# Weight places of 4128 instead of 4096 bytes in an attention and two-MLP kernel

## The chip, the cores and the metric

The kernel runs on one NeuronCore of a Trainium2 chip. The metric is the device time of one execution in microseconds. Three runs of the kernel before took 950.89, 951.58 and 952.81 us; the median is 951.58 us.

## What is computed

Linear attention with exponential features, and two MLPs behind it, all float32. The matmuls of the MLPs split each operand in two parts (high and low) that TensorE takes as `float32r`, and add three products.

```python
def phi(x):                                   # d_feat = 128
    proj = x @ w_phi
    proj = proj - max(abs(proj), axis=-1)
    return concat([exp(proj), exp(-proj)])
q_p, k_p = phi(q), phi(k)                     # q, k, v: 4 x 8 x 576 x 64
kv = einsum('bhsf,bhsd->bhfd', k_p, v); z = sum(k_p, axis=2)
x = einsum('bhsf,bhfd->bhsd', q_p, kv) / (einsum('bhsf,bhf->bhs', q_p, z) + 1e-6)
x = x.transpose(0, 2, 1, 3).reshape(2304, 512)
x = ((x @ w1) * (x @ w2)) @ w3 @ w_out        # d_ff = 1024
x = square(maximum(x @ w_in, 0)) @ w_out2     # d_ff = 2048
```

## The kernel before

Three stages follow each other on TensorE: attention (about the first 190 us), the first MLP (to about 550 us) and the second MLP (to the end). The 2304 rows are worked in four blocks of 512 columns (one for each batch) and one block of 256 columns, the tail rows of all batches (`mains`, `tail`, lines 787 to 789). Attention writes its rows to HBM, and the MLP blocks are loaded from there.

**The matmuls of the MLPs.** `passes` (line 155) gives the three pairs: high with high, low with high, high with low. `wide` (line 175) makes 12 matmuls: for each of four 128-row slices of the input three passes, with a slice of a weight tile as the stationary operand and a tile `c` of the input (512 columns) as the moving one. The first MLP runs `wide` for `pa` and `pb`, and `fold_in` (line 877) makes 12 matmuls `yp` with the folded weight `w3o` stationary and the gated product `g` moving. `w3o` is the product of w3 and w_out, 24 matmuls `pf` for each of eight slices (line 840, class `Fold`). One loop of the first MLP is `pa`, `pb` and the `yp` of the step before; there are two groups of four steps on each block. The second MLP runs `wide` for `ph` (a column tile of w_in stationary) and `last_product` (line 895) for `op`: there the squared activation `r` is stationary and the tile of w_out moves. One loop is `ph` of step j and `op` of step j - 1, 16 loops on each block.

**Behind a `ph`** ScalarE takes the relu (`t`, line 1035), VectorE the square (line 1037), ScalarE the high part of `r` (line 1043), VectorE the low part (line 1045); `op` needs `r` one loop later. The input tiles `c` and `y` are split the same way (`split`, lines 144 and 145).

**Where tiles lie.** All tiles lie in SBUF, with 128 partitions each, and sizes here are bytes of one partition. A tile of a weight is `[2, 512]` in 4 bytes, so 4096: the high part, then the low part. There are 20 places on the left side (`LEFT`, pool `units`, tag "u") and 12 on the right (`RIGHT`, pool `late`, tag "w"). `unit` (line 64) and `lunit` (line 708) hand them out; `take` (line 718) picks a side and falls to the other where the first has no free place, and `give`, `tick` and `home` keep the count. The same places also hold x and y tiles on their way from and to HBM. The `c` tiles have places of their own (`place`, line 67, pool `mid`, behind the left places); the `g` and `r` tiles share a tag of `late`, behind the right places. In the program as it is built, left place k begins at byte 43648 + 4096k, the `c` places at 125568 + 4096k, right place k at 159712 + 4096k, and the three places of `g` and `r` at 217056, 221152 and 225248. Counted modulo 64 that is 0, 0, 32 and 32. Between the left and the right pools 1376 bytes are free. In attention the matmuls `pk` (line 246) have a `c` place (offset 0) stationary and `wbd`, on the right at 189472 (offset 32), moving.

In the second MLP the w_in tiles (even numbers of `w_w2`) lie left, and the w_out tiles (odd numbers) lie right, but for the numbers 11, 13, 15 and 31, which lie left. At 668.88 us `op` takes number 11, at 674.42 number 13.

The order of the instructions on each engine is written out by hand (`START`, `SLOT`, the loops under `manual_schedule`).

Of the kernel before, what the change touches and what calls it, by code (L numbers as in the profile page):

```python
# [17 lines left out]
P = 128  # L18
C = 4
TAIL = 64  # L20
LEFT = 20
RIGHT = 12

# [18 lines left out]
def attention_then_mlps(ctx: ExitStack, tc: tile.TileContext, q, k, v, w_phi, w1, w2, w3, wo, wi2, wo2, out):  # L44
# [15 lines left out]
    units = ctx.enter_context(tc.tile_pool(name="units", bufs=1))  # L60
    mid = ctx.enter_context(tc.tile_pool(name="mid", bufs=1))
    dram = ctx.enter_context(tc.tile_pool(name="dram", bufs=1, space=bass.MemoryType.DRAM))

    def unit(dtype, shape, name):
        return units.tile([P] + shape, dtype, tag="u", bufs=LEFT, name=name)

    def place(i, name):

# [59 lines left out]
    def decode_splitting(src, name, got, tile_of=unit):  # L128
        w = []
        yield from decoding(src, name, w)  # L130
        dst = tile_of(F32R, [2, 512], f"w_{name}")
        yield
        nc.scalar.activation(dst[:, 0], w[0], AF.Copy)  # L133
        yield
        nc.gpsimd.tensor_tensor(out=dst[:, 1], in0=w[0], in1=dst[:, 0].bitcast(F32), op=ALU.subtract)  # L135
        got.append(dst)
# [38 lines left out]
    def wide(ps, n, w, cs, kks=range(KD)):  # L175
# [8 lines left out]
        (b, i): dram.tile([P, 2, C * P], F32, name=f"x_hbm_{b}_{i}") for b in range(B) for i in range(KD // 2)  # L184
    }
    xt = unit(F32, [KD, B * TAIL], "xt")
    y_hbm, x_in, y_in = {}, {}, {}

    def load_x(b):
        if b == B:  # L190
            x_in[b] = [xt[:, kk, :] for kk in range(KD)]
            return
        x_in[b] = []
        for i in range(KD // 2):
            xu = unit(F32, [2, C * P], f"x_{b}_{i}")
            nc.sync.dma_start(xu, x_hbm[b, i])
            x_in[b] += [xu[:, 0, :], xu[:, 1, :]]


    with ExitStack() as actx:  # L200
# [346 lines left out]
        def plan(kind, i):  # L547
            got = []
            if kind == "w3":
                return got, decoding(*w3_of(i), w3s), 0  # L550
            if kind == "w12":
                src, name = w12_of(i)
                return got, decode_splitting(src, name, w12, lambda *a: take(*a, side="u")), 1
            side = "w" if i % 2 else "u"
            return got, decode_splitting(w2_of(i), f"w2_{i}", got, lambda *a: take(*a, side=side)), 1
# [133 lines left out]
        with tc.manual_schedule(engines=mine):  # L689
            for entry in START:  # L690
                name, t = entry.split("/")
# [11 lines left out]
    late = ctx.enter_context(tc.tile_pool(name="late", bufs=2, side="right", reuse_waits="tile"))  # L703
# [2 lines left out]
    pre = ctx.enter_context(tc.tile_pool(name="pre", bufs=4, space=PSUM, reuse_waits="tile"))  # L706

    def lunit(dtype, shape, name, tag="w", bufs=RIGHT):
        return late.tile([P] + shape, dtype, tag=tag, bufs=bufs, name=name)

    def bank_of(pool, tag, name):
# [1 line left out]


    free = {"u": LEFT - 18, "w": RIGHT}
    home, given = {}, []

    def take(dtype, shape, name, side="w"):

        tag = side if free[side] else "uw".replace(side, "")  # L720
        assert free[tag] > 0, name
        free[tag] -= 1
        t = (lunit if tag == "w" else unit)(dtype, shape, name)
        home[t.name] = tag
        return t

    def give(*ts):
        given.extend(home.get(t.name, "u") for t in ts)

    def tick():  # L730
        while given:
# [60 lines left out]
    def load_x_at(b):  # L792
        if b == B:
            x_in[b] = [xt[:, kk, :] for kk in range(KD)]
            return []
        us = [take(F32, [2, C * P], f"x_{b}_{i}_{len(blocks)}") for i in range(KD // 2)]
        for i, xu in enumerate(us):
            nc.sync.dma_start(xu, x_hbm[b, i])
        x_in[b] = [xu[:, s, :] for xu in us for s in range(2)]
        return us  # L800
# [9 lines left out]
    class Fold:  # L810
# [22 lines left out]
        def product(self):  # L833
            self.pf = pf = bank_of(pre, "pre", f"pf_{self.kc}")
            for g in range(2):
                t = self.t[g]
                for j in range(4):
                    sl, wj = slice(j * P, (j + 1) * P), wos[4 * g + j]
                    for n, (a, c) in enumerate(passes((t[:, 0, sl], t[:, 1, sl]), (wj[:, 0], wj[:, 1]))):
                        nc.tensor.matmul(pf, a, c, start=g + j + n == 0, stop=g == 1 and j == 3 and n == 2)  # L840
            give(*self.t)
            if self.kc == NG - 1:
                give(*wos)
# [13 lines left out]
    def evict_first(b, n, yp):  # L857
        us = [take(F32, [2, n], f"y_{b}_{i}") for i in range(KD // 2)]
        for i, y in enumerate(us):
            nc.scalar.copy(y[:, 0, :], yp[2 * i][:, 0:n])  # L860
            nc.vector.tensor_copy(y[:, 1, :], yp[2 * i + 1][:, 0:n])
            y_part[b, i] = dram.tile([P, 2, n], F32, name=f"y_part_{b}_{i}")
            nc.sync.dma_start(y_part[b, i], y)
        give(*us)
# [52 lines left out]
    with tc.manual_schedule(engines=mine):  # L917
# [5 lines left out]
        for s, (grp, at, k) in enumerate(steps):  # L923
# [7 lines left out]
            b, n = blk.b, blk.n  # L931
# [16 lines left out]
            if s == 0:  # L948
                g = first["g"]
            else:  # L950
                pa = bank_of(pre, "pre", f"pa_{b}_{c}")
                wide(pa, n, w12[2 * c], blk.cs)
                a_sb = lunit(F32, [512], f"a_{b}_{c}", "t", 2)
                nc.scalar.copy(a_sb[:, 0:n], pa[:, 0:n])  # L954
                pb = bank_of(pre, "pre", f"pb_{b}_{c}")
                wide(pb, n, w12[2 * c + 1], blk.cs)
                if at == B:
                    give(w12[2 * c], w12[2 * c + 1])
                if k == HG - 1:
                    col_split(x_in[nb_], nn, f"c{s}_{nb_}", [1, 2])  # L960
                g32 = lunit(F32, [512], f"g32_{b}_{c}", "g32", 2)
                nc.vector.tensor_tensor(out=g32[:, 0:n], in0=pb[:, 0:n], in1=a_sb[:, 0:n], op=ALU.mult)  # L962
                g = lunit(F32R, [2, 512], f"g_{b}_{c}", "g", 3)
                nc.scalar.activation(g[:, 0, 0:n], g32[:, 0:n], AF.Copy)  # L964
                beat.one()
                nc.vector.tensor_tensor(
                    out=g[:, 1, 0:n], in0=g32[:, 0:n], in1=g[:, 0, 0:n].bitcast(F32), op=ALU.subtract
                )
                if k == HG - 1:
                    nxt = col_split(x_in[nb_], nn, f"c{s}_{nb_}", [3])  # L970
                    give(*coming)
                    if nb_ == B and following[0] == 1:
                        give(xt)
# [39 lines left out]
        for at, (b, n) in enumerate(mlp2):  # L1013
            cs, nt = nxt, n // P
            ops = None
            for j in range(NR):
# [17 lines left out]
                t = lunit(F32, [512], f"t_{b}_{j}", "t", 2)  # L1034
# [58 lines left out]
```

## Time and profile before

| what | value |
| --- | --- |
| median of 3 runs | 951.58 us (950.89 to 952.81) |
| span of the profiled execution | 952.7 us (its own time isn't listed apart) |
| TensorE matmuls busy | 931.8 us, 98% of the span |
| TensorE weight loads busy | 764.0 us, 80% (beside the matmuls) |
| VectorE busy | 545.8 us, 57% |
| ScalarE busy | 382.4 us, 40% |
| GpSimd busy | 249.5 us, 26% |
| mean granted clock of TensorE | 0.998 |
| DMA | 94 GB/s in the mean, 16 engines together |

The profile is of one execution. "PE" is the matmuls of TensorE, "PEld" its weight loads; "busy" joins what overlaps, and a matmul's duration overlaps with that of the next. In the order of time, equal instructions that follow each other on an engine are one row: start, duration of the whole row, and the number of instructions at the end. The spacing of matmuls is read from the starts of successive rows. Buffer numbers are left out of names, so `w_w` is any weight tile of the second MLP, whatever place it has.

### The profile page before, as it was taken

The numbers are of one execution on the slowest core, as the hardware profiler recorded it, in microseconds if no ns is written. First come the engines' busy times: TensorE is split into PE (matmuls) and PEld (weight loads), VectorE is DVE, ScalarE is ACT, GpSimd is POOL, SyncE is SP. The second block draws the span as 40 slices with busy tenths as digits, with TensorE's granted clock in tenths as the row PEclk, the third lists the DMA queues.
The fourth block names the chain that finished last, engine by engine and source line by source line (L and its number), as shares of the span: only waits on it lengthen the run. The fifth ranks groups of instructions, "written<-read, shape, count | busy, mean of one in ns | idle before, by whom it ended". The sixth has DMA issues, their size and how long they took to land.

```text
span 952.7 us, 14857 instructions
## 1 busy us (share of the span) xinstructions
PE 931.8 (98%) x5915; PEld 764.0 (80%) x5915; DVE 545.8 (57%) x892; ACT 382.4 (40%) x689; POOL 249.5 (26%) x304
## 2 busy tenths in 40 slices
PE   8899998999999999999999999999999999999997
PEld 7677776778888988888988888888888888888896
DVE  5898889778656456666856678852224223322332
ACT  4777777643322333432333344342223223222322
POOL 1565566454121123333423245520000000000000
PEclk9999999999999999999999999999999999999999
DMA  6565566144241334254452333211002000100000
GB/s 166 125 159 151 136 158 199 55 153 157 87 133 55 124 110 155 67 199 155 164 187 91 132 126 96 89 41 48 1 1 89 1 0 1 67 1 1 29 17 22
DMA packets 81109, 89.22 MB, mean 94 GB/s; under 512 B 44624, under 2 KB 65680, under 8 KB 81040
## 3 DMA queue, kind: packets, MB, share of 16 engines
q1 hardware_dynamic: 79712, 87.72, 29.7%
q8 instruction: 46, 0.75, 0.3%
q10 hardware_dynamic: 1328, 0.56, 0.3%
q14 instruction: 23, 0.19, 0.1%
HBM read 69.76 MB, written 18.35 MB: 92 GB/s over the span
## 4 chain that ended last, share of the span: by engine, by line
PE 89%; DVE 4%; ACT 3%; DMA 2%; issue 1%; SPq 0%; ACTq 0%
PE op L901 21%; PE ph L179 21%; PE yp L883 11%; PE pb L179 10%; PE pa L179 10%; PE pf L840 5%; PE po L455 2%; PE pk L246 2%; PE pq L376 2%; PE pkv L428 2%; DMA mrow<-mh 2%; ACT qp L417 2%; PE pd L477 1%; DVE kmax L344 1%; DVE m L383 1%; ACT kp L361 1%
## 5 line engine op out<-in xcount | busy, mean ns | idle before, releaser
L901 PE MATMUL op<-w_w,r 128*128 128x512 f32 x864 | 213.8, 395 | 0.1
L901 PEld LDWEIGHTS op<-w_w,r 128*128 128x128 f32 x864 | 161.3, 188 | 36.8 <-ACT r L1043 0.5
L179 PE MATMUL ph<-y,w_w 128*128 128x512 f32 (+1 forms) x768 | 165.5, 365 | 0.0
L1037 DVE SCALAR_TENSOR_TENSOR r<-ph,t 128x512 f32<-128x512 f32 (+1 forms) x80 | 51.0, 638 | 194.0 <-ACT t L1035 194.0
L179 PEld LDWEIGHTS ph<-y,w_w 128*128 128x128 f32 x768 | 133.3, 188 | 25.8
L1035 ACT ACTIVATE t<-ph 128x512 f32<-128x512 f32 (+1 forms) x80 | 44.5, 556 | 222.2 <-PE ph L179 222.2
L883 PE MATMUL yp<-g,w3o 128*128 128x512 f32 (+1 forms) x480 | 107.6, 373 | 0.0
L883 PEld LDWEIGHTS yp<-g,w3o 128*128 128x128 f32 x480 | 83.8, 188 | 16.0
L125 POOL TENSOR_TENSOR dt_w<-dt_w,dy_w 128x512 f32<-128x512 f32 x48 | 62.9, 1310 | 126.8 <-DVE dy_w L120 126.7
L179 PE MATMUL pa<-c,w_w12a 128*128 128x512 f32 (+1 forms) x432 | 94.4, 368 | 0.0
L179 PE MATMUL pb<-c,w_w12b 128*128 128x512 f32 (+1 forms) x432 | 93.6, 366 | 0.0
L179 PEld LDWEIGHTS pa<-c,w_w12a 128*128 128x128 f32 x432 | 75.1, 188 | 14.2
L179 PEld LDWEIGHTS pb<-c,w_w12b 128*128 128x128 f32 x432 | 75.2, 189 | 13.0
L1045 DVE TENSOR_TENSOR r<-r,r 128x512 fp32r<-128x512 f32 (+1 forms) x80 | 51.0, 638 | 41.3 <-ACT r L1043 35.6
L962 DVE TENSOR_TENSOR g<-pb,a 128x512 f32<-128x512 f32 (+1 forms) x39 | 24.8, 636 | 85.9 <-PE pb L179 81.3
L135 POOL TENSOR_TENSOR w_w<-dt_w,w_w 128x512 fp32r<-128x512 f32 x32 | 48.9, 1528 | 86.8 <-ACT w_w L133 86.8
L1043 ACT ACTIVATE r<-r 128x512 fp32r<-128x512 f32 (+1 forms) x80 | 47.2, 590 | 55.5 <-DVE r L1037 55.5
L502 POOL TENSOR_SCALAR rc<-dc 32x9 f32<-32x9 f32 x128 | 45.4, 355 | 58.8 <-DVE dc L492 51.8
L964 ACT ACTIVATE g<-g 128x512 fp32r<-128x512 f32 (+1 forms) x39 | 23.0, 589 | 91.6 <-DVE g L962 91.6
L954 ACT COPY a<-pa 128x512 f32<-128x512 f32 (+1 forms) x39 | 21.2, 543 | 83.1 <-PE pa L179 83.1
L361 ACT ACTIVATE kp<-kp 128x512 f32<-128x512 f32 (+1 forms) x80 | 46.9, 588 | 17.2 <-DVE kp L354 14.8
L117 DVE TENSOR_SCALAR dy_w<-dt_w 128x512 int32<-128x512 int32 x48 | 51.1, 1064 | 0.7
(135 smaller groups left out, 1285.3 us busy)
## 6 DMA issues: line engine op xcount, KB each, us to landing
x<-x_hbm SPq DMA_DIRECT2D x16, 512.0 KB
raw_w<-in_moe_w_dram SPq DMA_DIRECT2D x16, 512.0 KB
raw_w<-in_moe_w_in_dram SPq DMA_DIRECT2D x16, 512.0 KB
raw_w<-in_moe_w_out_dram SPq DMA_DIRECT2D x16, 512.0 KB
qm<-in_q_dram SPq DMA_DIRECT2D x32, 128.0 KB
km<-in_k_dram SPq DMA_DIRECT2D x16, 256.0 KB
vs<-in_v_dram SPq DMA_DIRECT2D x32, 128.0 KB
raw_wo<-in_moe_w_out_dram SPq DMA_DIRECT2D x8, 512.0 KB
```

What stands on the lines that cost most here:

```text
L117: nc.vector.tensor_scalar(out=e, in0=t, scalar1=-(1 << 23), scalar2=None, op0=ALU.bitwise_and)
L125: nc.gpsimd.tensor_tensor(out=w, in0=t.bitcast(F32), in1=e.bitcast(F32), op=ALU.add)
L135: nc.gpsimd.tensor_tensor(out=dst[:, 1], in0=w[0], in1=dst[:, 0].bitcast(F32), op=ALU.subtract)
L179: nc.tensor.matmul(ps[:, 0:n], a, c, start=kk + i == 0, stop=kk == KD - 1 and i == 2)
L361: nc.scalar.activation(z["kp", j][:, :, s, :], z["kp", j][:, :, 1, :], AF.Exp, scale=1.0 - 2.0 * s)
L502: nc.gpsimd.tensor_scalar(out=z["rc2"][i * 32:(i + 1) * 32, s, :], in0=z["dc"][at * 32:(at + 1) * 32, :], scalar1=1e-6, scalar2=None, op0= ...
L840: nc.tensor.matmul(pf, a, c, start=g + j + n == 0, stop=g == 1 and j == 3 and n == 2)
L883: nc.tensor.matmul(blk.yp[i][:, 0:blk.n], a, d, start=c % HG + s == 0, stop=c % HG == HG - 1 and s == 2)
L901: nc.tensor.matmul(ops[i], a, d, start=j + s == 0, stop=j == NR - 1 and s == 2)
L1037: nc.vector.scalar_tensor_tensor(out=r32[:, 0:n], in0=ph[:, 0:n], scalar=0.0, in1=t[:, 0:n], op0=ALU.max, op1=ALU.mult)
L1043: nc.scalar.activation(r[:, 0, 0:n], r32[:, 0:n], AF.Copy)
L1045: nc.vector.tensor_tensor(out=r[:, 1, 0:n], in0=r32[:, 0:n], in1=r[:, 0, 0:n].bitcast(F32), op=ALU.subtract)
```

## The change

Each weight place takes 4128 bytes: a flat tile of 1024 + 8 words is asked for, and the first 1024 words are handed on, in the shape that was asked for. Left place k so begins at 43648 + 4128k and the right places, whose pool ends where it did, at 159328 + 4128k. The `c` places move by 20 x 32 = 640 bytes; `g`, `r`, `a`, `g32` and `t` tiles stay. Since what `unit` and `lunit` return is now a part of a tile, `home` is kept by the names that the kernel gives, found through `names`.

```diff
+SPACE = 8
+    def spaced(pool, shape, dtype, tag, bufs, name):
+        n = 1
+        for d in shape:
+            n *= d
+        t = pool.tile([P, 1024 + SPACE], dtype, tag=tag, bufs=bufs, name=name)
+        ap = t[:, 0:n]
+        if len(shape) > 1:
+            ap = ap.rearrange("p (a n) -> p a n", a=shape[0])
+        return ap
+
     def unit(dtype, shape, name):
-        return units.tile([P] + shape, dtype, tag="u", bufs=LEFT, name=name)
+        return spaced(units, shape, dtype, "u", LEFT, name)
...
     def lunit(dtype, shape, name, tag="w", bufs=RIGHT):
+        if tag == "w":
+            return spaced(late, shape, dtype, tag, bufs, name)
         return late.tile([P] + shape, dtype, tag=tag, bufs=bufs, name=name)
...
-    home, given = {}, []
+    home, given, names = {}, [], {}
...
-        home[t.name] = tag
+        home[name] = tag
+        names[id(t)] = t, name
         return t
 
     def give(*ts):
-        given.extend(home.get(t.name, "u") for t in ts)
+        given.extend(home.get(names.get(id(t), (t, ""))[1], "u") for t in ts)
```

## Rows read from the trace of the kernel before

**Rows 1.** The page: engine, busy us, share, instructions; then the chain by engine.
```profile
PE 931.8 (98%) x5915; PEld 764.0 (80%) x5915; DVE 545.8 (57%) x892; ACT 382.4 (40%) x689; POOL 249.5 (26%) x304
...
PE 89%; DVE 4%; ACT 3%; DMA 2%; issue 1%; SPq 0%; ACTq 0%
```

**Rows 2.** Busy time by engine, clock and DMA share between 550 and 902 us.
```profile
core 0: us, PE busy (x) PEld busy (x) DVE busy (x) ACT busy (x) POOL busy (x), PEclk, DMA share, GB/s
550.00:902.00 352.00, 352.00 (x1532) 286.90 (x1531) 142.41 (x207) 104.44 (x179) 38.49 (x28) 1.00 0.11 38
```

**Rows 3.** TensorE in order of time, second MLP: start us, duration us, what.
```profile
660.57 2.92 PE L179 MATMUL ph<-y,w_w 128*128 128x512 f32 x12
663.34 2.94 PE L901 MATMUL op<-w_w,r 128*128 128x512 f32 x12
666.11 2.93 PE L179 MATMUL ph<-y,w_w 128*128 128x512 f32 x12
668.88 2.97 PE L901 MATMUL op<-w_w,r 128*128 128x512 f32 x12
671.68 2.90 PE L179 MATMUL ph<-y,w_w 128*128 128x512 f32 x12
674.42 2.97 PE L901 MATMUL op<-w_w,r 128*128 128x512 f32 x12
677.22 2.90 PE L179 MATMUL ph<-y,w_w 128*128 128x512 f32 x12
```

**Rows 4.** The same view, one loop of the first MLP.
```profile
353.46 2.92 PE L179 MATMUL pa<-c,w_w12a 128*128 128x512 f32 x12
356.22 2.88 PE L179 MATMUL pb<-c,w_w12b 128*128 128x512 f32 x12
358.94 2.94 PE L883 MATMUL yp<-g,w3o 128*128 128x512 f32 x12
361.72 2.92 PE L179 MATMUL pa<-c,w_w12a 128*128 128x512 f32 x12
```

**Rows 5.** The chain that ended last, in order of time: start us, us, what.
```profile
657.96 2.78 PE op L901 x12
...
669.04 2.81 PE op L901 x12
```

**Rows 6.** TensorE in order of time: a fold and the run after it.
```profile
218.45 5.64 PE L840 MATMUL pf<-w_wo,w3T 128*128 128x512 f32 x24
223.93 2.88 PE L179 MATMUL pa<-x,w_w12a 128*128 128x512 f32 x12
```

**Rows 7.** The same view: eleven matmuls of 256 columns, and what follows.
```profile
46.60 1.46 PE L246 MATMUL pk<-wbd,kT 128*128 128x256 f32 x11
47.90 0.27 PE L284 MATMUL pkt<-ident,km 128*128 128x128 f32 x1
...
57.11 1.47 PE L246 MATMUL pk<-wbd,kT 128*128 128x256 f32 x11
58.42 0.60 PE L284 MATMUL pkt<-ident,km 128*128 128x128 f32 x4
...
905.96 1.47 PE L179 MATMUL ph<-y,w_w 128*128 128x256 f32 x11
907.27 0.40 PE L901 MATMUL op<-w_w,r 128*128 128x512 f32 x1
```

**Rows 8.** Groups by line and form, 550 to 902 us: busy us, mean ns | idle before.
```profile
L1045 DVE TENSOR_TENSOR r<-r,r 128x512 fp32r<-128x512 f32 x64 | 44.2, 691 | 33.5 <-ACT r L1043 33.2
L1043 ACT ACTIVATE r<-r 128x512 fp32r<-128x512 f32 x64 | 40.5, 633 | 47.6 <-DVE r L1037 47.6
L145 DVE TENSOR_TENSOR y<-yi,y 128x512 fp32r<-128x512 f32 x12 | 8.5, 706 | 2.3 <-ACT y L144 2.3
L144 ACT ACTIVATE y<-yi 128x512 fp32r<-128x512 f32 x12 | 7.5, 621 | 2.2 <-PE ph L179 2.2
```

**Rows 9.** All engines in order of time: the low part of `r`.
```profile
665.62 0.69 DVE L1045 TENSOR_TENSOR r<-r,r 128x512 fp32r<-128x512 f32 x1 [0.70 <-ACT r L1043]
```

## The prediction

> **What bounds the kernel now.** I read the page's busy times and the chain first: TensorE is busy for 98% of the span and the chain of work that ended last is 89% TensorE [rows 1]. Then the table by stages: between 550 and 902 us TensorE is busy for 352.00 of 352.00 us, while VectorE has 142 and ScalarE 104, and the granted clock is 1.00, the upper of the two levels, 2.4 GHz [rows 2]. So nothing is waited for there. What sets the time is how closely one matmul follows another, and each nanosecond of spacing goes straight into the end. The change moves weight tiles in SBUF, and no instruction is added or taken away; so the question is whether the spacing depends on where the tiles lie. I therefore read the order of time of TensorE alone, where each row is a run of 12 matmuls of 512 columns and the differences of the starts are what counts (the durations overlap).
>
> In the second MLP a loop is 12 `ph` and 12 `op` matmuls. From 660.57 to 666.11 it takes 5.54 us: `ph` 2.77, `op` 2.77 [rows 3]. From 671.68 to 677.22 it takes 5.54 too, but split as 2.74 and 2.80 [rows 3]. In the first MLP a loop is `pa`, `pb`, `yp`: from 353.46 on they take 2.76, 2.72 and 2.78, together 8.26 [rows 4]. The least of these, 2.72 us for 12, is 226.7 ns for a matmul; call it the floor. Against it a loop of the second MLP loses 5.54 - 24 x 0.2267 = 0.10 us, and so does one of the first: 8.26 - 36 x 0.2267 = 0.10.
>
> Why do equal instructions take 2.72 to 2.80? I laid the rows beside the places that the built program gives the tiles. Left weight places, and the `c` places, begin at a multiple of 64 bytes; right weight places and the `g`/`r` places begin 32 bytes past one. `pb` streams a left `c` under a left weight, as `pa` just before it did: the floor. `yp` streams a right `g` under a right weight, `pa` and `ph` go back to left under left: 0.04 to 0.06 us over the floor for 12, a cost of changing over. Most `op` runs stream a right weight under a right `r`; those at 668.88 and 674.42 (four in each block: tiles 11, 13, 15 and 31) stream a left weight under a right `r`, and these take 2.80, 0.08 over the floor, where the run after them takes 2.74 [rows 3]. So two operands that stand 32 bytes apart, counted modulo 64, keep a worse spacing, about 7 ns for each matmul.
>
> The Trainium skill says otherwise: "TensorE: Matmul & The Clock Gate", Part 2, step 1, has it that TensorE has two independent read ports, so that loading the next weights takes no read bandwidth from the running matmul; by that rule places can't matter, and the time would stay. The rows above, the same instruction at 2.77 and 2.80, don't agree with it.
>
> **The change part by part.**
> *Weight places, left (20) and right (12).* Place k moves by 32k bytes, so that its offset modulo 64 alternates between 0 and 32. `c` places move by 640 bytes, a multiple of 128, and `g`, `a`, `g32` stay: the partner of each weight keeps its offset and the weights don't. Every other weight place stops matching its partner if the period is 64 bytes, three in four if it is 128, nearly all if it is longer. The trace shows only two offsets, 0 and 32 modulo 64, so the period is unknown and so is the spacing at 64 or 96 bytes.
> Price if a run doesn't match: 2.80 us by the starts [rows 3], 2.81 in the chain, where a matched `op` has 2.78 [rows 5]; I take 2.805, or 0.085 over the floor, 7.1 ns x 12. If all stopped matching, a loop of the second MLP would go from +0.10 to 2 x 0.085 = +0.17, that is +0.07, on 4 blocks x 16 = 64 loops of 512 columns: 4.5 us. A loop of the first MLP would go from +0.10 to 3 x 0.085 = 0.255, +0.155, on 2 x 4 x 4 = 32 loops: 5.0 us. The eight folds `pf` take 5.48 for 24 matmuls, 0.04 over the floor [rows 6]; unmatched 2 x 0.085 = 0.17, +0.13 each: 1.0 us. Sum: 10.5 us for all; half of it, 5.3, for a period of 64; three quarters, 7.9, for 128.
> From below: if all runs of 12 came to the floor, the changing over would be gone: 64 x 0.10 + 32 x 0.10 + 8 x 0.04 = 9.9 us less. So the bounds are -9.9 and +10.5. I take +5.3: 32 against 0 modulo 64 is the only difference that the rows show a price for, and it gives half.
> *The blocks of 256 columns* (the tail rows): eleven matched `ph` take 1.31 us, 119 ns each, and in attention eleven `pk`, whose operands stand 32 bytes apart, take 1.30 or 1.31 [rows 7]: not matching costs nothing there. One or two ns on some 400 matmuls is under 1 us either way; I count 0.
> *Other engines and DMAs that use the moved tiles.* VectorE on `r` (32 past a multiple of 64) takes 691 ns, on `c` (a multiple of 64) 706; ScalarE 633 and 621 [rows 8]: no price for 32 bytes. VectorE has the last part of `r` at 665.62 + 0.69 = 666.31 [rows 9], and the `op` that needs it starts at 668.88 [rows 3]; even some 100 ns more on each of the four steps would sit in these 2.57 us. If that cover went, it would be late at every loop, 64 times. The DMAs into moved tiles keep their size, queue (SP) and order; the DMA engines are busy 0.11 of that stage [rows 2].
> *Bookkeeping* (`home`, `names`): Python only, nothing is issued. No wait is added, and no queue is passed.
>
> The sum is against the profiled span, 952.7 us, all of whose MLP part is spacing; it goes to the run times as a difference. The median of the runs is 951.58, 1.1 below the span: 951.6 + 5.3 = 956.9 us.
>
> **The rivals.**
> *A longer period, or an offset worse than 32 bytes:* almost no weight matches: +8 to +10.5, some 961 us. For it: only 0 is known to reach the floor. Against: nothing shows a difference between 32 and 96.
> *Nothing changes:* what matters is not the low bits but something that goes with left and right, which the change leaves. In the trace of before every tile low in memory has offset 0 and every tile high in memory 32, so the two can't be told apart. Against: `c` places and left weight places lie far apart and still match, and a border would have to fall just between the `c` places and the first right place. 951.6 us. That the change didn't do what it says ends here too: if the allocator rounded a place up to a multiple of 64 bytes or more; but places of 2080 bytes stand in the program now, and the 1024 bytes more fit into the 1376 that are free between left and right.
> *Faster:* places that differ let the two read streams pass each other. The mechanism: the price is paid when the weights' offset changes between runs (0 to 32 and back), not while it differs. A loop has two such changes now; with half of the left weights at offset 32, as `r` has it, half of the second MLP's loops have none: 32 x 0.10 = 3.2 us, and a share of the first MLP's, another 1 to 2. That is 947 us; in the limit of the floor for all, 941.7. For it: both kinds of `op` loop lose the same 0.10 although one of them doesn't match for half its length [rows 3]; and `pk`, 32 bytes apart, is no dearer than the matched `ph` of 256 columns [rows 7]. Against: the run that doesn't match has 2.80, the dearest of all, as a run. It decides as soon as loops with one weight offset throughout cost less than 0.05.
>
> **How the numbers follow.** Unmatched at half to three quarters of the places (+4 to +9): 0.45, forecast 956.9, its own range 955 to 961. Worse than that: 0.13. Nothing: 0.17. Faster: 0.25. A measurement of this kernel tells about 0.2% (1.9 us) from no change; so slower 0.58, same 0.17, faster 0.25. The range takes the first case whole, the bulk of the second, the third and the nearer half of the fourth: 946 to 963.
>
> **What would show it.** In the changed kernel the runs of 12 `ph`, `pa` and `pb` should fall into kinds by the parity of the left place: about 2.73 to 2.77 and 2.80 to 2.81; `op` and `yp` likewise by the right place. Loops of 5.54 and 8.26 should become 5.54 to 5.62 and 8.26 to 8.42. If all runs keep 2.72, 2.76 and 2.78, low bits don't matter. If some kinds fall under 2.72, the floor isn't one, and the forecast has the wrong sign. The busy times of the other engines and the granted clock should stay; if VectorE's or ScalarE's mean on `r`, `w` or `y` tiles moves by over 5%, I am wrong on them.

## The result and the profile after

The changed kernel takes 958.73 us (median of 4 runs, 958.51 to 958.99), the kernel before 952.19 us in the same four rounds (the three runs listed ahead and a fourth of 953.87): a ratio of 1.007, with a 95% interval of 1.0055 to 1.0085. It is 6.5 us slower, 5.2 to 8.1 by the interval; forecast were 5.3.

The page of the changed kernel, busy us by engine, share and instructions: the same instructions as in [rows 1], and TensorE busy for 5.7 us more.

```profile
PE 937.5 (98%) x5915; PEld 762.8 (80%) x5915; DVE 546.0 (57%) x892; ACT 382.8 (40%) x689; POOL 249.6 (26%) x304
```

TensorE of the changed kernel in order of time, second MLP (start us, duration us, what); it answers to [rows 3]:

```profile
569.24 2.89 PE L190 MATMUL ph<-c,w_w 128*128 128x512 f32 x12
571.97 2.95 PE L915 MATMUL op<-w_w,r 128*128 128x512 f32 x12
574.76 2.95 PE L190 MATMUL ph<-c,w_w 128*128 128x512 f32 x12
577.54 2.96 PE L915 MATMUL op<-w_w,r 128*128 128x512 f32 x12
580.34 2.97 PE L190 MATMUL ph<-c,w_w 128*128 128x512 f32 x12
583.15 2.96 PE L915 MATMUL op<-w_w,r 128*128 128x512 f32 x12
```

From start to start these runs of 12 take 2.73, 2.79, 2.78, 2.80 and 2.81 us. In the kernel before there were two kinds of `ph` and two of `op`; now there is one for nearly every place. The first MLP, against [rows 4]:

```profile
353.92 2.97 PE L190 MATMUL pa<-c,w_w12a 128*128 128x512 f32 x12
356.73 2.96 PE L190 MATMUL pb<-c,w_w12b 128*128 128x512 f32 x12
359.53 2.95 PE L897 MATMUL yp<-g,w3o 128*128 128x512 f32 x12
362.32 2.91 PE L190 MATMUL pa<-c,w_w12a 128*128 128x512 f32 x12
```

`pa` 2.81, `pb` 2.80, `yp` 2.79: a loop of 8.40 where there was one of 8.26. `pb`, which stood at the floor, lost most. A fold, against [rows 6], takes 5.58 where it took 5.48:

```profile
217.20 5.74 PE L854 MATMUL pf<-w_wo,w3T 128*128 128x512 f32 x24
222.78 2.98 PE L190 MATMUL pa<-x,w_w12a 128*128 128x512 f32 x12
```

Where the time came from is read over whole stretches. The kernel before: 14 loops of the first MLP between the first two of these rows, and 16 loops of the second from the third to the `ph` at 660.57 [rows 3].

```profile
336.94 2.92 PE L179 MATMUL pa<-c,w_w12a 128*128 128x512 f32 x12
452.58 2.92 PE L179 MATMUL pa<-c,w_w12a 128*128 128x512 f32 x12
571.93 2.93 PE L179 MATMUL ph<-c,w_w 128*128 128x512 f32 x12
```

The changed kernel, the same loops; the last row ends the 16 loops that begin at 574.76:

```profile
337.11 2.96 PE L190 MATMUL pa<-c,w_w12a 128*128 128x512 f32 x12
454.46 2.96 PE L190 MATMUL pa<-c,w_w12a 128*128 128x512 f32 x12
663.85 2.95 PE L190 MATMUL ph<-y,w_w 128*128 128x512 f32 x12
```

The 14 loops went from 115.64 to 117.35, 0.122 us a loop: 3.9 us for 32. The 16 loops went from 88.64 to 89.09: 4 x 0.45 = 1.8 us for four blocks. The folds add 8 x 0.10 = 0.8. That would be 6.5 us together, but it is carried over from one stretch of each kind. The two profiles also show the MLPs whole, from the first fold to the last 12 `op`. In the kernel before:

```profile
203.75 5.74 PE L840 MATMUL pf<-w_wo,w3T 128*128 128x512 f32 x24
943.97 3.50 PE L901 MATMUL op<-w_w,r 128*128 128x512 f32 x12
```

and in the changed kernel:

```profile
202.27 5.83 PE L854 MATMUL pf<-w_wo,w3T 128*128 128x512 f32 x24
948.25 3.50 PE L915 MATMUL op<-w_w,r 128*128 128x512 f32 x12
```

From start to start that is 740.22 and 745.98 us: the MLPs cost 5.8 us more. With the starts of all runs laid side by side, 3.8 of them are in the first MLP's runs of 512 columns, 1.8 in those of the second MLP and 0.7 in the folds; the 40 runs of 12 matmuls with 256 columns give 0.5 back. The other 0.7 us of the difference of the medians isn't located; 5.8 too lies in the interval. (The spans of the two profiled executions, 952.7 and 956.8, differ by only 4.1, since in the second attention was 1.5 us ahead at the first fold. Such differences come with the execution: the one kernel of e1 and e10 below is 1.05 us ahead there in one profile and 1.59 in the other, against the kernel before.)

VectorE and ScalarE didn't move: on `r` and `y` they have the means of [rows 8] within 2 ns:

```profile
L1059 DVE TENSOR_TENSOR r<-r,r 128x512 fp32r<-128x512 f32 x63 | 43.5, 691 | 33.1 <-ACT r L1057 32.8
L1057 ACT ACTIVATE r<-r 128x512 fp32r<-128x512 f32 x63 | 39.8, 633 | 47.2 <-DVE r L1051 47.2
L156 DVE TENSOR_TENSOR y<-yi,y 128x512 fp32r<-128x512 f32 x12 | 8.5, 706 | 2.3 <-ACT y L155 2.3
L155 ACT ACTIVATE y<-yi 128x512 fp32r<-128x512 f32 x12 | 7.5, 623 | 2.2 <-PE ph L190 2.2
```

To find which offsets cost, each run of 12 of 512 columns after 330 us (199 of them) was laid beside the places of its two operands in the built program. d is the place of the stationary tile less that of the moving one, modulo 256; the time is from the run's start to the next one's.

| d, bytes | runs in the changed kernel | mean us | least and most |
| --- | --- | --- | --- |
| 0 | 22 | 2.737 | 2.721 to 2.755 |
| 32 | 26 | 2.793 | 2.785 to 2.803 |
| 64 | 24 | 2.795 | 2.789 to 2.803 |
| 96 | 22 | 2.800 | 2.790 to 2.810 |
| 128 | 34 | 2.796 | 2.784 to 2.801 |
| 160 | 30 | 2.799 | 2.790 to 2.807 |
| 192 | 21 | 2.765 | 2.743 to 2.800 |
| 224 | 20 | 2.796 | 2.786 to 2.802 |

Taken modulo 512 the two halves of each class agree within 0.01 us, but for 192 (2.754 and 2.773); taken modulo 128 they don't (0 and 128, 64 and 192). Within a run of 12 the offset is the same throughout, for the tile that is being loaded as for the one that is in use, so the table doesn't tell which of the two reads pays. In the kernel before 183 of the 199 runs have d = 0, and 16, the `op` runs with a left weight, have 96. So the theory for the experiments is: TensorE keeps its floor where both operands begin at the same offset modulo 256; any other difference costs up to 0.09 us for 12 matmuls; and going over from one offset to another costs a little by itself. Its rivals: a shorter period (64 or 128), a cost that belongs to left and right and not to low bits, and the spacing of places as such.

### The profile page after: what moved, and what is told of

The parts are those of the page before. It is cut to its first block, busy times and chain, and to the rows that moved or that the text cites. A ratio compares the mean times of both kernels' runs of the same rounds, so it can differ in the third digit from the quotient of the medians.

```text
span 956.8 us, 14857 instructions
## 1 busy us (share of the span) xinstructions
PE 937.5 (98%) x5915; PEld 762.8 (80%) x5915; DVE 546.0 (57%) x892; ACT 382.8 (40%) x689; POOL 249.6 (26%) x304
## 4 chain that ended last, share of the span: by engine, by line
PE 90%; DVE 4%; ACT 2%; DMA 2%; issue 1%; SPq 0%; ACTq 0%
PE op L915 21%; PE ph L190 21%; PE pb L190 11%; PE yp L897 11%; PE pa L190 10%; PE pf L854 5%; PE po L466 2%; PE pk L257 2%; PE pq L387 2%; PE pkv L439 2%; DMA mrow<-mh 2%; ACT qp L428 1%; PE pd L488 1%; DVE kmax L355 1%; ACT kp L372 1%; DVE m L394 1%
```

## The experiments

### All places at one offset

The left side is moved by 96 bytes (e1), which makes left weights, `c`, right weights, `g` and `r` alike modulo 256. The other tiles on the left move with them; nothing else differs from the kernel before.

```diff
-    ident = const.tile([P, P], F32, name="ident")
+    ident = const.tile([P, P + 24], F32, name="ident")[:, 0:P]
```

> The kernel before, with every tile on the left (weights, c) 96 bytes further, so that left weights, c, right weights, g and r all begin at the same offset modulo 256 (224). Period of 256 bytes, and only the offset of the stationary to the moving operand counts: all runs of 12 take 2.72 us, no cost of changing over is left, loops 5.44 and 8.16 us, 941 to 943 us. Changing over between left and right costs something by itself: loops stay at 5.54 and 8.26, 951.6 us. Low bits don't count at all: 951.6 us.

943.97 us, a ratio to the kernel before of 0.9908 (0.9889 to 0.9927). TensorE in order of time, first and second MLP:

```profile
354.52 2.88 PE L179 MATMUL pb<-c,w_w12b 128*128 128x512 f32 x12
357.24 2.88 PE L883 MATMUL yp<-g,w3o 128*128 128x512 f32 x12
359.96 2.88 PE L179 MATMUL pa<-c,w_w12a 128*128 128x512 f32 x12
...
663.12 2.88 PE L901 MATMUL op<-w_w,r 128*128 128x512 f32 x12
665.84 2.88 PE L179 MATMUL ph<-y,w_w 128*128 128x512 f32 x12
```

Every run takes 2.72, also the `op` at 663.12 with a left weight, tile 11, which took 2.80 [rows 3]. So neither left and right nor going over between them costs anything once the offset is the same. That left weight stands at 224 modulo 512 here and its `r` at 480, so a period of 512 is ruled out too. The stretch of 16 loops is 87.04, which is 32 x 2.72. The median is a little above the 941 to 943 expected. This kernel beats both; the same kernel was measured again on another occasion (e10):

> The same kernel as in e1_left96, for a narrower interval: 941 to 945 us, a ratio of 0.989 to 0.993 to the kernel before.

943.08 us against 952.53, 0.9907 (0.9887 to 0.9926).

### Which period

The same edit with 8 words (32 bytes, e2), which makes left and right alike modulo 64 only, and with 56 words (224 bytes, e3), alike modulo 128 but not 256.

```diff
+    ident = const.tile([P, P + 8], F32, name="ident")[:, 0:P]      # 32 bytes
+    ident = const.tile([P, P + 56], F32, name="ident")[:, 0:P]     # 224 bytes
```

> As the first, but 32 bytes further: left and right places are now alike modulo 64 and differ by 64 modulo 128 and 256. Period 64: as good as the first, 941 to 943 us. Period 128 or 256: left under left and right under right match as in the kernel before, the changing over stays, 950 to 954 us; the four op runs of a block with a left weight stay at about 2.80 us.

948.78 us, 0.9967 (0.9955 to 0.998). TensorE in order of time:

```profile
656.69 2.89 PE L179 MATMUL ph<-y,w_w 128*128 128x512 f32 x12
659.42 2.92 PE L901 MATMUL op<-w_w,r 128*128 128x512 f32 x12
662.18 2.89 PE L179 MATMUL ph<-y,w_w 128*128 128x512 f32 x12
664.92 2.96 PE L901 MATMUL op<-w_w,r 128*128 128x512 f32 x12
667.71 2.91 PE L179 MATMUL ph<-y,w_w 128*128 128x512 f32 x12
```

> As the first, but 224 bytes further: left and right places are alike modulo 128 and differ by 128 modulo 256. Period 64 or 128: 941 to 943 us. Period 256: 950 to 954 us, the op runs with a left weight at about 2.79 us.

945.44 us, 0.9937 (0.9917 to 0.9958). TensorE in order of time:

```profile
656.44 2.89 PE L901 MATMUL op<-w_w,r 128*128 128x512 f32 x12
659.17 2.89 PE L179 MATMUL ph<-y,w_w 128*128 128x512 f32 x12
661.90 2.96 PE L901 MATMUL op<-w_w,r 128*128 128x512 f32 x12
664.70 2.92 PE L179 MATMUL ph<-y,w_w 128*128 128x512 f32 x12
```

The `op` with the left weight (664.92 and 661.90) takes 2.79 and 2.80: 64 bytes apart and 128 bytes apart don't match, so the period is neither 64 nor 128. Both kernels are nevertheless faster than the 950 to 954 us that a period of 256 was thought to give, and the rows say why: going over has become cheaper. `ph` and `op` after it take 2.73 and 2.76 where left and right differ by 64, and 2.73 and 2.73 where they differ by 128; by 96, in the kernel before, they take 2.77 and 2.77. That the cost of going over depends on the distance was in no theory; a loop of the second MLP loses 0.10 us at 96 bytes, 0.05 at 64, 0.02 at 128, nothing at 0.

### The offset alone, with the weight places as they were

A tile of 96 bytes ahead of the `c` places (e4); the weight places keep their 4096 bytes.

```diff
+    pad = mid.tile([P, 24], F32, tag="pad", bufs=1, name="pad")
+    nc.gpsimd.memset(pad, 0.0)
```

> The kernel before with the c places alone 96 bytes further; all weight places stay 4096 bytes apart. If the offset of weight to c counts: every pa, pb and ph of 512 columns takes 2.79 to 2.81 us where it had 2.76, 2.72 and 2.76; loops of the second MLP about 5.58, of the first about 8.38: +6 us, 957 to 959 us. If it is the spacing of 4096 bytes between weight places, or left against right, that counts: 951.6 us.

957.11 us, 1.0057 (1.0035 to 1.0079): with nothing spaced, a loss like that of the change (1.007). TensorE in order of time:

```profile
356.74 2.96 PE L181 MATMUL pa<-c,w_w12a 128*128 128x512 f32 x12
359.54 2.96 PE L181 MATMUL pb<-c,w_w12b 128*128 128x512 f32 x12
362.34 2.01 PE L885 MATMUL yp<-g,w3o 128*128 128x512 f32 x8
```

`pa` and `pb` take 2.80 each, where they took 2.76 and 2.72 [rows 4]; `ph` likewise takes 2.79 to 2.80.

### Spacing alone, with the offset kept

The other way round (e9): all places alike modulo 256 (the shift of 96 bytes), and the `c` places 4352 bytes apart, 17 x 256.

```diff
-        return mid.tile([P, 2, 512], F32R, tag=f"c{min(i, 2)}", bufs=1 if i < 2 else 3, name=name)
+        t = mid.tile([P, 1024 + 64], F32R, tag=f"c{min(i, 2)}", bufs=1 if i < 2 else 3, name=name)
+        return t[:, 0:1024].rearrange("p (a n) -> p a n", a=2)
```

> The kernel with all places alike modulo 256, but its five c places 4352 bytes apart (17 x 256), so that they still are alike modulo 256. If the offset modulo 256 is what counts: all runs of 12 at 2.72 us, as with 4096, 941 to 945 us. If places that aren't a power of two apart cost by themselves: pa, pb and ph slower, over 948 us.

941.69 us, 0.9891 (0.9868 to 0.9914). Runs of 12 in order of time:

```profile
657.96 2.88 PE L902 MATMUL op<-w_w,r 128*128 128x512 f32 x12
660.67 2.88 PE L180 MATMUL ph<-y,w_w 128*128 128x512 f32 x12
663.39 2.88 PE L902 MATMUL op<-w_w,r 128*128 128x512 f32 x12
```

2.71 and 2.72: `c` places that aren't 4096 bytes apart cost nothing if they stay alike modulo 256. Weight places of 4352 bytes don't fit: 32 x 256 = 8192 bytes more, where 1376 are free. They were not tried.

### Each side of the change alone

The first kernel (e5) leaves the spacing of the right places out, the second (e6) that of the left ones.

```diff
-        if tag == "w":
-            return spaced(late, shape, dtype, tag, bufs, name)
```
```diff
-        return spaced(units, shape, dtype, "u", LEFT, name)
+        return units.tile([P] + shape, dtype, tag="u", bufs=LEFT, name=name)
```

> The change on the 20 left places alone; right places stay 4096 bytes apart. By the price read from the changed kernel (ph 2.78 for 2.76, pb 2.79 for 2.72, pa 2.80 for 2.76, op and yp nearly as before): most of the loss, 956 to 958 us. By the forecast's sum, in which every run that doesn't match costs the same: some two thirds of it, about 955 us.

953.88 us against 951.2: 1.0027 (1.0009 to 1.0045). TensorE in order of time:

```profile
656.89 2.91 PE L913 MATMUL op<-w_w,r 128*128 128x512 f32 x12
659.63 2.95 PE L190 MATMUL ph<-y,w_w 128*128 128x512 f32 x12
662.42 2.90 PE L913 MATMUL op<-w_w,r 128*128 128x512 f32 x12
665.16 2.96 PE L190 MATMUL ph<-y,w_w 128*128 128x512 f32 x12
```

> The change on the 12 right places alone; left and c as before. op and yp lose the match, but they already paid for changing over (2.78): 951.5 to 953.5 us. By the forecast's sum: a third of the loss, about 954 us.

950.57 us against 951.2: 1.0002 (0.9978 to 1.0025), no difference. TensorE in order of time:

```profile
656.39 2.89 PE L190 MATMUL ph<-y,w_w 128*128 128x512 f32 x12
659.12 2.97 PE L915 MATMUL op<-w_w,r 128*128 128x512 f32 x12
661.92 2.90 PE L190 MATMUL ph<-y,w_w 128*128 128x512 f32 x12
```

The parts don't add up to the whole: 2.7 and 0 against 6.5 us; in the MLPs of the profiles, from the first fold on, 2.4 and 0.4 against 5.8. Of the figures expected for the left side, 956 to 958 failed; the other, about 955, lies inside the interval (0.9 to 4.3 us over the kernel before). Where one side no longer matches, many runs of the other side get cheaper: with the left places alone spaced `op` takes 2.74 for 2.77, and with the right ones alone `op` takes 2.80 but `ph` 2.73 and 2.74 for 2.77. It isn't a rule, though. By the places in the built program, `ph` of the second kernel takes 2.72 to 2.74 after an `op` with a d of 32, 64 or 96, but 2.76 to 2.77 after one of 128 to 224, as after one that matches. And in the first kernel the `c` places have moved by 640 bytes, which is 128 modulo 256, so that they stand 32 bytes from `r` modulo 256 where they stood 96; the four `op` runs there that match and follow a matching `ph` take 2.74 as well. Which of the two made `op` cheaper wasn't separated. With both sides spaced few runs are left that match (22 of 199), so little can be handed back. The 16 loops of the second MLP show it: 88.64 before, 88.57 with the left side, 88.64 with the right side, 89.09 with both.

### A difference of 16 bytes

The kernel with `c` places of 4352 bytes, and `c` itself 16 (e7) or 240 bytes (e8) into its place; `op` and `yp` have equal offsets, `pa`, `pb` and `ph` a d of 240 and of 16.

```diff
-        return t[:, 0:1024].rearrange("p (a n) -> p a n", a=2)
+        return t[:, 4:4 + 1024].rearrange("p (a n) -> p a n", a=2)       # 16 bytes; 60 for 240
```

> The kernel with all places alike modulo 256, but c places 4352 bytes apart (17 x 256) and c itself 16 bytes into its place. op and yp of equal offset on both operands, pa, pb and ph with 240 between weight and c. If every difference that isn't a multiple of 256 costs: these at 2.75 to 2.81, 945 to 951 us. If the floor of 2.72 comes from the two reads meeting, a small shift could go under it: ph under 2.72, below 942 us.

951.62 us, 1.0002 (0.9979 to 1.0026). In order of time:

```profile
657.40 2.91 PE L902 MATMUL op<-w_w,r 128*128 128x512 f32 x12
660.15 2.94 PE L180 MATMUL ph<-y,w_w 128*128 128x512 f32 x12
662.92 2.91 PE L902 MATMUL op<-w_w,r 128*128 128x512 f32 x12
```

> The same with c 240 bytes into its place, so that the weight is 16 bytes ahead of c modulo 256. Every difference costs: 2.75 to 2.81 for pa, pb, ph, 945 to 951 us; a small shift helps: below 942 us.

951.58 us, 0.9999 (0.9981 to 1.0018). In order of time:

```profile
657.73 2.88 PE L902 MATMUL op<-w_w,r 128*128 128x512 f32 x12
660.45 2.96 PE L180 MATMUL ph<-y,w_w 128*128 128x512 f32 x12
663.25 2.88 PE L902 MATMUL op<-w_w,r 128*128 128x512 f32 x12
```

Neither shift goes under the floor. `ph` takes 2.77 with d = 240 and 2.80 with d = 16, and either kernel loses what the equal offset had won, 9 to 10 us against the kernel with `c` places of 4352 bytes; that is above the 945 to 951 expected, by a little. The two aren't mirror images: with 240 `op` takes 2.75 though its own operands match, with 16 it takes 2.72.

## Why the prediction was right

*What bounds the kernel.* Right. In the MLPs nothing but the spacing of matmuls moved, and it accounts for 5.8 of the 6.5 us; the rest is inside the interval.

*That places count.* Right, and shown by moving single pools: e4 takes the spacing away and keeps the unequal offset, and has the loss; e9 keeps a spacing and makes the offset equal, and has none. The rule of the Trainium skill ("TensorE: Matmul & The Clock Gate", Part 2, step 1: two independent read ports, so that loading weights takes nothing from the running matmul) would make all of these kernels alike if it meant that places can't matter, as the prediction took it. Runs of the same 12 matmuls at 2.72 and 2.80 us speak against that reading, and the measurement decides. Why TensorE behaves so stays open: no trace shows SBUF reads, nor whether it is the load or the running matmul that pays.

*The price of a run that doesn't match.* 0.085 us over the floor, taken from one kind of run at d = 96. Measured 0.073 to 0.080 for six of the seven differences and 0.045 for 192. A little too high.

*How many stop matching: the step that failed.* The prediction took every other place, since 32 against 0 modulo 64 was the only difference with a price. But that price came from tiles 96 bytes apart modulo 256. The period is 256, and 177 of 199 runs stopped matching, nine in ten; `c`, which moved by a multiple of 128 but not of 256, left its partners too. The rival with a longer period named that, but priced it at +8 to +10.5; the measured +6.5 lies between. Two errors of opposite sign met, too few runs at too high a price, so that the forecast of the whole came as near as it did by luck. Term by term, half of the forecast's sum against the profile: second MLP 2.2 against 1.8, first MLP 2.5 against 3.8, folds 0.5 against 0.7. The first MLP is the term that was too small: `pb` had nothing to hand back, since it paid no going over. In the second MLP a loop's +0.07 was the difference of 0.17 and 0.10; the 16 loops show 89.09 / 16 - 5.44 = 0.13 in place of 0.17, which leaves 0.03.

*The blocks of 256 columns.* Counted at nothing, with under 1 us either way: 0.5 us less by the profile. Not matching costs nothing there: in e4, 32 of these runs stand 96 bytes apart and take 1.43 us for 12, as the matching ones did before.

*The sign on the parity of places.* "By the parity of the left place" was wrong with the period: there are as many kinds as d has values.

*Other engines and DMAs.* Right: the same means.

*The rival "faster".* Its limit, all runs at the floor for 9.9 us less, is what e1, e9 and e10 reached (8 to 11 us less), but by equal offsets, not by different ones. Its mechanism, that the price is paid when the weights' offset changes and not while it differs, fell: in e4 `pb` follows `pa` with the same offsets of weight and `c`, and takes 2.80 like it.

## What to carry to other kernels

Where TensorE is the bound, lay the two operands of the matmuls out alike: in this kernel a shift of 96 bytes for one side of SBUF, so that stationary and moving tiles begin at equal offsets modulo 256, was worth 0.9%, and places of 4128 instead of 4096 bytes cost 0.7%. This was seen on float32r matmuls of 512 columns; those of 256 columns showed no price. Look for it in the starts of successive matmuls of equal form: if equal instructions come at two or more spacings, always the same ones, sort them by where their operands lie before looking for waits. And when an offset between tiles is to be changed, ask what it is measured against; padding the tiles of one operand moves each of them against its partner.

## What had not been expected of the hardware

- The offset modulo 256 of the stationary against the moving operand sets the spacing of float32r matmuls of 512 columns: 226.7 ns with equal offsets (2.72 us for 12), 233 ns with most others (2.79 to 2.80), about 230 at 192 bytes. In matmuls of 256 columns no such price shows.
- After going over from one offset to another, matmuls are slower although their own operands match: in the kernel before nine of the twelve spacings of a matching `op` run are 229 to 236 ns in the mean, where those of `pb` are 226 to 228. How much it costs depends on the distance: 0.10 us a loop for 96 bytes, 0.05 for 64, 0.02 for 128.
- Tiles 16 bytes apart are about as bad as tiles 32 bytes apart: 2.80 us with a d of 16, 2.77 with 240, 2.79 with 32.
